# Attention in front of two expert layers: transposes on row halves, fp32 scores without parts, both products with v in one PSUM tile

## The chip, the cores and the metric

One core of a Trainium2 chip runs the whole program. The metric is the device time of one execution in microseconds; the median of three runs of the kernel before is 954.91 us (954.55 to 956.79).

## The reference

Three layers follow each other; only the first is touched by the change.

```python
B, H, S, D = q.shape                       # 4, 8, 576, 64
scores = q @ k^T / sqrt(D); scores = where(causal, -1e9, scores)
a = softmax(scores); local = a @ v
q_p = phi(q)                               # elu(q) + 1
mem_out = (q_p @ M_prev) / (q_p . z_prev + 1e-6)
g = sigmoid(beta)                          # per head
x = (g * mem_out + (1 - g) * local) -> [B*S, H*D] = [2304, 512]
...
# then: each token through one of 8 experts (512 -> 1024 -> 512), weighted by its gate,
# then elu(x @ w_in) @ w_out (512 -> 2048 -> 512)
```

## The kernel before, in words

The program has three stages, each planned and emitted by `Plan`: attention (with the routing of tokens to experts mixed in), the experts, the last layer. A stage is written as operations with an engine or a choice of engines, a cost, what they read and write, and a priority; `Plan.order` (L156) walks through time, gives each engine the next operation that is ready, hands out buffers from rings of fixed size, and so fixes the order of instructions on each engine. On the chip each engine then runs its list in that order. The costs are numbers in the source (`TICK`, `DRAIN`, `HOP`, and one per operation); the priorities are in the table `KNOBS`, `off` above all.

Attention goes through 16 pairs of heads (`pair(p)` in `attention`): 4 batches x 4 pairs. All its PSUM use goes through one ring of four buffers of 1024 fp32 columns, called `pat` in the trace (`c.rx`, two banks each). Per pair:

1. `load` (L543) brings q, k, v of both heads, 128 tokens to a row tile, so that a tile has 128 tokens x (2 heads x 64).
2. `tr` (L561) transposes k and q on TensorE, five 128x128 blocks each (L570), into PSUM: 128 partitions (2 heads x 64) x tokens.
3. `parts` (L574) reads these and writes two float32r parts of each, high and low: `ha` or `hv` (L584, L587) and a subtraction on VectorE (L591). `ends` (L632) copies the last 64 columns of q into a block-diagonal array (L641).
4. `phi_in` and the GpSimd step (L604 to L629) make phi(q).
5. `scores` (L653): row tiles of 128 queries i = 0 to 3, and a last one of 64 queries, both heads in one tile. Each score is a sum of three float32r matmuls, high x high, low x high, high x low (L667; L678 for the last tile). The two heads stand in the two halves of the array's rows. The causal mask is added by small bf16 matmuls (L671, L679). VectorE takes the row minimum (L687; scores are negated), ScalarE the exponential with its row sum (L692).
6. `weights` (L696): the weights are transposed on TensorE in 128x128 blocks (L705), 2, 4, 6, 8 and 5 of them for the five row tiles, and copied out of PSUM (`evac`, L515) into `aA` (tiles 0 to 2) and `aB` (tiles 3 and 4).
7. A matmul with `swap` (L750) brings one row sum to the other half; VectorE makes the factors (L754 to L762).
8. `quarters` (L522) multiplies phi(q) with the memory (64x64 quarters of the array, four at once), and later the transposed result with an identity to bring it back (same line).
9. The products with v (L806): 384 tokens from `aA`, 192 from `aB`, the two heads in the two halves of the array's columns, each group in its own PSUM buffer and copied on its own (`evac` to `xT`).
10. VectorE scales (L791, L826), GpSimd adds into the row of x (L838).

After each batch `gate_plan` computes which expert each token goes to (a table by 20 bf16 matmuls, L945, among others), and `routing` the places of the first tiles.

Of the kernel before, what the change touches and what calls it, by code (L numbers as in the profile page):

```python
# [18 lines left out]
P = 128  # L19
# [5 lines left out]
NI = 5  # L25
# [59 lines left out]

class Plan:
# [10 lines left out]
    DRAIN = 90.0  # L97
# [129 lines left out]
    "xe": ("ACT", "DVE"), "he": ("ACT",), "re": [("ACT",), ("ACT", "DVE")], "m_ld": 3500.0, "m_x": -2208.9, "m_1": -1447.9, "m_h": -4434.5,  # L227
    "m_lag": 0.0, "m_if": 700.0, "m_fl": -3000.0, "m_wl": 300.0, "wa": 0, "wa0": 10022.449169040721, "wa1": 23927.854833523612, "wt": 1, "wp": 16, "wj": 2000.0,
    "m_g": -500, "wq": 0.64, "sa": 60.0, "sm": 50.0, "s2": 0.0, "step": -68438.62, "hd": -241.62,
    "mem": 379947.52, "xg": 4,  # L230
# [242 lines left out]
def attention(tc, ctx, c, q, k, v, M_prev):  # L473
# [28 lines left out]
    r_aA, r_aB = sb("aA", 2, [P, 2, 896]), sb("aB", 2, [P, 2, NI, 192])  # L502
# [12 lines left out]
    def evac(n, dst, src, **kw):  # L515
# [5 lines left out]
        pl.op(("ACT", "DVE"), (ca(n), cv(n)), (fa, fv), **kw)  # L521
# [9 lines left out]
    def pair(p):  # L531
# [8 lines left out]

        def load(slot, src, lo, eng="SP"):
# [8 lines left out]
        load(sqi, q, D)  # L550
        load(ski, k, 0, "ACT" if p == 0 else "SP")
# [5 lines left out]
        def row(y):  # L557
            return sab.t[:, y * QW:(y + 1) * QW]

        def diag(x):  # L560
            return sab.t[:, 4 * QW + P * x:4 * QW + P * (x + 1)]  # L561
        xq, xk = [(Slot(rx), 0, QW)], [(Slot(rx), 0, S)]

        def tr(xs, s):
            pt = at("tk" if s is ski else "tq")
            for x, n0, n1 in xs:
                def mk(x, n0, n1):
                    def f():
# [3 lines left out]
                    pl.op("PE", 109 * -(-(n1 - n0) // P), f, r=[s], w=[x] + [(y, "own", n0) for y in ([sab] if s is ski else [sab, se, sqT])], prio=pt)  # L572
                mk(x, n0, n1)

        def parts(xs, hi, lo, scale):
            for x, n0, n1 in xs:
                def mk(x, n0, n1):
                    n = n1 - n0

                    def to(y):  # L580
                        return row(y)[:, n0:n1]

                    def ha():
                        nc.scalar.activation(to(hi), x.t[:, 0:n], AF.Copy, scale=scale)  # L584

                    def hv():
                        nc.vector.tensor_scalar_mul(to(hi), x.t[:, 0:n], scale)  # L587
                    pl.op(("ACT", "DVE"), (ca(n), cv(n)), (ha, hv), r=[x, (x, 0)], w=[(sab, hi)], prio=at("hi"))

                    def f():  # L590
                        nc.vector.scalar_tensor_tensor(to(lo), x.t[:, 0:n], scale, to(hi).bitcast(F32), op0=ALU.mult, op1=ALU.subtract)  # L591
                    pl.op("DVE", cv(n), f, r=[x, (sab, hi)], w=[(sab, lo), (x, 0)], prio=at("lo"))
                mk(x, n0, n1)

# [4 lines left out]
        parts(xk, 0, 2, 1.0)  # L599
        xq0 = xq[0][0]  # L600

        def phi_in():
            def f():
                nc.scalar.activation(se.t, xq0.t[:, 0:QW], AF.Exp)  # L604
            pl.op("ACT", ca(QW), f, r=[xq0], w=[se, (xq0, 0)], prio=at("px"))

            def f():
                nc.scalar.activation(sqT.t[:, 0:512], xq0.t[:, 0:512], AF.Relu)
            pl.op("ACT", ca(512), f, r=[xq0], w=[(sqT, 0), (xq0, 0)], prio=at("px"))

# [6 lines left out]
        parts(xq, 1, 3, -0.125)  # L617
# [3 lines left out]
        for n, n0, n1, m0 in ((0, 0, 512, 0), (1, 512, S, S)):  # L621
            def mk(n, n0, n1, m0):
                def fv():
                    nc.vector.scalar_tensor_tensor(sqT.t[:, n0:n1], se.t[:, m0:m0 + n1 - n0], 1.0, sqT.t[:, n0:n1], op0=ALU.min, op1=ALU.add)

                def fp():
                    e = se.t[:, m0:m0 + n1 - n0]
                    nc.gpsimd.tensor_scalar(e, e, 1.0, 0.0, op0=ALU.min, op1=ALU.add)  # L628
                    nc.gpsimd.tensor_tensor(sqT.t[:, n0:n1], e, sqT.t[:, n0:n1], op=ALU.add)  # L629
                es, m = K["qe"], n1 - n0  # L630
                pl.op(es, [{"DVE": cv(m), "POOL": cps(m) + cpt(m)}[x] for x in es], [{"DVE": fv, "POOL": fp}[x] for x in es], r=[se], w=[(sqT, n), (se, "phi", n)], prio=at("phi"))
            mk(n, n0, n1, m0)  # L632
# [64 lines left out]
        def weights(i, hs, js, ps):  # L697
# [12 lines left out]
            def dst():  # L710
# [3 lines left out]
                if i == 3:  # L714
                    return sB.t[:, h, j0:j1, 0:P]
# [1063 lines left out]
```

## Time and profile before

| what | value |
|---|---|
| median of three runs | 954.91 us |
| the profiled execution | 954.44 us, its span 952.7 us |
| PE (TensorE matmuls) busy | 921.3 us, 97% |
| PEld (TensorE weight loads) busy | 770.3 us, 81% |
| DVE (VectorE) busy | 639.2 us, 67% |
| ACT (ScalarE) busy | 446.9 us, 47% |
| POOL (GpSimd) busy | 179.6 us, 19% |
| granted TensorE clock, mean | 0.991 |

A line of the profile names engine, source line and operation, then output <- inputs by the program's names. For a TensorE line the pair like 64\*128 is the rows and columns of the array in use, and the next one the partitions and moving columns. An fp32 matmul that is not a transpose stands in the trace as two instructions, a float32r one, a bf16 one and a transpose as one. Matmuls are pipelined: a start-to-start distance is what one costs, its own length is more.

### The profile page before, as it was taken

What the parts mean: (1) busy time and instruction counts of PE and PEld (TensorE: products, weight loads), DVE (VectorE), ACT (ScalarE), POOL (GpSimd) and SP (SyncE); (2) the same over time, 40 slices, a digit from 0 to 9 for tenths busy, and PEclk for the clock granted to TensorE, in tenths of its full rate; (3) what the DMA queues carried; (4) which work ended last, traced back from release to release, by engine and by line L of the source; (5) the groups of instructions that cost most, each with busy time, mean ns of one, the idle gap of its engine ahead of it and who ended that gap; (6) DMA issues with size and microseconds to landing.
All of it is one profiled execution on the core that took longest, in us unless ns stands there. A gap on an engine that the chain in (4) does not pass through costs nothing. (4 is left out here: it accounts for less than half of the span.)

```text
span 952.7 us, 18441 instructions
## 1 busy us (share of the span) xinstructions
PE 921.3 (97%) x6858; PEld 770.3 (81%) x6858; DVE 639.2 (67%) x1179; ACT 446.9 (47%) x902; POOL 179.6 (19%) x244
## 2 busy tenths in 40 slices
PE   9998998999899999999999999999999999999996
PEld 6777887778678888888878789988888888888895
DVE  3878878887775568646898596555565556555553
ACT  3787778767454347536866562222122221212211
POOL 3344442434300122222321100010001000100100
PEclk8999999989999999999999999999999999999999
DMA  6333433243632697569997370110011000100000
GB/s 124 79 75 84 94 75 103 64 147 132 221 122 88 228 343 250 170 225 361 331 335 279 125 242 1 34 45 1 1 45 45 1 12 23 45 0 1 20 26 23
DMA packets 96597, 110.00 MB, mean 115 GB/s; under 512 B 64879, under 2 KB 64879, under 8 KB 94193
## 3 DMA queue, kind: packets, MB, share of 16 engines
q1 hardware_dynamic: 90496, 95.25, 31.4%
q0 software_dynamic: 4800, 13.18, 3.8%
q8 instruction: 55, 0.90, 0.4%
q10 hardware_dynamic: 1200, 0.30, 0.2%
q14 instruction: 46, 0.37, 0.1%
HBM read 87.94 MB, written 23.41 MB: 117 GB/s over the span
## 5 line engine op out<-in xcount | busy, mean ns | idle before, releaser
L1588 ACT ACTIVATE elu<-pt 128x512 f32<-128x512 f32 x72 | 43.1, 598 | 266.0 <-PE pt L1580 266.0
L1613 PE MATMUL pt<-w,gh 128*128 128x512 f32 x432 | 134.2, 392 | 0.5 <-DVE gh L1492 0.5
L1380 PE MATMUL pm<-w,hh 128*128 128x512 f32 x368 | 125.1, 401 | 0.8 <-ACT y L1393 0.8
L1596 DVE TENSOR_SCALAR elu<-elu 128x512 f32<-128x512 f32 x72 | 30.8, 428 | 127.1 <-ACT elu L1588 127.1
L1613 PEld LDWEIGHTS pt<-w,gh 128*128 128x128 f32 x432 | 79.6, 188 | 16.3 <-DVE gh L1492 0.9
L692 ACT ACTIVATE a<-pat,st 128x128 f32<-128x128 f32 (+2 forms) x144 | 78.0, 550 | 22.5 <-DVE st L687 18.3
L1613 PE MATMUL pt<-w,gl 128*128 128x512 f32 x216 | 84.3, 390 | 0.0
L1380 PEld LDWEIGHTS pm<-w,hh 128*128 128x128 f32 x368 | 69.2, 188 | 14.5 <-ACT y L1393 1.2
L1380 PE MATMUL pm<-w,hl 128*128 128x512 f32 x184 | 71.9, 391 | 0.3 <-DVE hl L1214 0.3
L687 DVE TENSOR_REDUCE st<-pat 128x2 f32<-128x256 f32 (+4 forms) x80 | 63.8, 806 | 9.6 <-PE pat L671 9.6
L1580 PE MATMUL pt<-yTh,w 128*128 128x256 f32 (+1 forms) x288 | 69.2, 319 | 0.0
L705 PE MATMUL pat<-ident,a 128*128 128x128 f32 x400 | 56.9, 287 | 8.6 <-ACT a L692 8.4
L628 POOL TENSOR_SCALAR ex<-ex 128x512 f32<-128x512 f32 (+1 forms) x32 | 37.8, 1182 | 131.0 <-ACT ex L604 118.5
L705 PEld LDWEIGHTS pat<-ident,a 128*128 128x128 f32 x400 | 44.6, 145 | 16.0 <-ACT a L692 15.0
L1600 DVE SCALAR_TENSOR_TENSOR tnh<-tnh,elu 128x512 f32<-128x512 f32 x72 | 49.6, 690 | 7.7 <-ACT tnh L1592 1.8
L1337 PE MATMUL pm<-w,x 128*128 128x512 f32 x216 | 51.9, 392 | 1.3 <-DVE w L1214 0.9
L1495 DVE TENSOR_TENSOR gl<-tnh,gh 128x512 fp32r<-128x512 f32 x72 | 49.6, 691 | 4.2
L1580 PEld LDWEIGHTS pt<-yTh,w 128*128 128x128 f32 x288 | 49.2, 190 | 4.0
L1604 DVE SCALAR_TENSOR_TENSOR tnh<-pt,tnh 128x512 f32<-128x512 f32 x72 | 49.6, 690 | 3.3
L1337 PEld LDWEIGHTS pm<-w,x 128*128 128x128 f32 x216 | 40.2, 188 | 10.3 <-DVE w L1214 1.4
L1214 DVE TENSOR_TENSOR hl<-pm,hh 128x512 fp32r<-128x512 f32 x46 | 31.4, 684 | 25.0 <-ACTq L1311 14.4
L1613 PEld LDWEIGHTS pt<-w,gl 128*128 128x128 f32 x216 | 40.5, 188 | 9.0 <-DVE gl L1495 0.4
(342 smaller groups left out, 2107.3 us busy)
## 6 DMA issues: line engine op xcount, KB each, us to landing
wraw<-in_moe_w_dram SPq DMA_DIRECT2D x24, 1024.0 KB, 7.9
wrbw<-in_moe_w_dram SPq DMA_DIRECT2D x12, 1024.0 KB, 8.1
wide<-in_moe_w_in_dram SPq DMA_DIRECT2D x16, 512.0 KB, 5.4
wf<-half SPq DMA_DIRECT2D x32, 256.0 KB, 3.2
wide<-in_moe_w_out_dram SPq DMA_DIRECT2D x16, 512.0 KB, 5.8
wide<-wf SPq DMA_DIRECT2D x9, 512.0 KB, 5.3
q<-in_q_dram SPq DMA_DIRECT2D x32, 128.0 KB, 3.1
v<-in_v_dram SPq DMA_DIRECT2D x32, 128.0 KB, 2.5
```

The source lines that it names most:

```text
L628: nc.gpsimd.tensor_scalar(e, e, 1.0, 0.0, op0=ALU.min, op1=ALU.add)
L687: nc.vector.tensor_reduce(ss.t[:, 2 * i:2 * i + (2 if i < 4 else 1)], src(), axis=AX.X if i < 4 else AX.XY, op=ALU.min)
L692: nc.scalar.activation(sa[i].t[:, h, :] if i < 4 else sa[4].t[:, 0:S].rearrange("p (y n) -> p y n", y=2), src()[:, h, :] if i < 4 else src ...
L705: nc.tensor.transpose(w.t[:, y:y + P], t[:, j * P:(j + 1) * P], c.ident)
L1337: nc.tensor.matmul(g[hf].t, a.t[:, cc, :], b[:, 512 * hf:512 * (hf + 1)], start=(cc == 0 and n == 0), stop=(cc == 3 and n == 2))
L1380: nc.tensor.matmul(y.t, a.t[:, 2 * (q % 2) + jj, :], b[:, 512 * jj:512 * (jj + 1)], start=(q == 0 and jj == 0 and n == 0), stop=(q == 3 an ...
L1495: nc.vector.tensor_sub(lo(), src(), hi().bitcast(F32))
L1580: nc.tensor.matmul(h.t[:, n * j + n0:n * j + n1], w(cc, a, ft), b(cc), start=(cc == 0 and x == 0), stop=(cc == 3 and x == 2))
L1588: nc.scalar.activation(se.t, h.t, AF.Exp)
L1600: nc.vector.scalar_tensor_tensor(st.t, st.t, 0.0, se.t, op0=ALU.min, op1=ALU.mult)
L1604: nc.vector.scalar_tensor_tensor(st.t, h.t, 0.0, st.t, op0=ALU.max, op1=ALU.add)
L1613: nc.tensor.matmul(acc[a].t, y.t[:, n * j + P * a:n * j + P * (a + 1)], wsub(1, k, ft // 2)[:, ft % 2, :], start=(ft == 0 and x == 0), sto ...
```

## The change

- q and k are loaded 64 tokens to a row tile: tokens 0 to 319 in partitions 0 to 63, tokens 320 to 575 in 64 to 127 (`halves`, four DMAs each).
- All transposes of attention go over 64 rows at a time (`turn`): a block of 64 tokens x 128 columns becomes 128 x 64, the two row halves in turn, each into its own PSUM bank.
- Scores are one fp32 matmul in place of three float32r ones, over the columns that exist (128 where 256 stood for the first tile). The low parts, the padded arrays and the block-diagonal copies go. The last tile works in two 64x64 quarters at a time.
- Both products with v go into one PSUM buffer, with the swap matmul in two halves between them, and are copied by one operation of 576 columns.
- phi(q) is made by operations of 576 columns in place of 512 and 64.
- `weights` are copied by engines that the table `es` names; the order of attention is planned anew.

```diff
+TURN = 32.5
+def turn(nc, out, x, ident, z):
+    hs = slice(z * D, (z + 1) * D)
+    nc.tensor.transpose(out, x, ident[hs, hs])
...
-    DRAIN = 90.0
+    DRAIN = 95.0
...
+    "es": {"x": ("ACT",), "T0": ("ACT", "DVE"), "T3": ("ACT", "DVE"), "k": ("DVE",), "T1": ("ACT",), "T4": ("ACT", "DVE"), "q": ("ACT",), "T2": ("ACT",)},
...
+                for h in range(2):
+                    e.dma_start(t[0:D, :, h, :], src[b, h0 + h, 0:n, :].rearrange("(i p) d -> p i d", p=D))
+                    e.dma_start(t[D:P, 0:NI - 1, h, :], src[b, h0 + h, n:S, :].rearrange("(i p) d -> p i d", p=D))
...
-                        for i in range(n0 // P, -(-n1 // P)):
-                            nc.tensor.transpose(x.t[:, i * P - n0:(i + 1) * P - n0], s.t[:, i, :, :].rearrange("p h d -> p (h d)"), c.ident)
+                for i in range(NI):
+                    for z in range(2 if i < NI - 1 else 1):
+                        n = 512 * z + (i - NI * (1 - z)) * D + 512 * (1 - z)
+                        turn(nc, x.t[:, n:n + D], s.t[z * D:(z + 1) * D, i, :, :].rearrange("p h d -> p (h d)"), c.ident, z)
...
-                        nc.vector.scalar_tensor_tensor(to(lo), x.t[:, 0:n], scale, to(hi).bitcast(F32), op0=ALU.mult, op1=ALU.subtract)
+                nc.scalar.activation(row(y), at_tokens(x), AF.Copy, scale=scale)
...
-                for k, (x, y) in enumerate(((0, 1), (2, 1), (0, 3))):
-                    for h in range(2):
-                        hs = slice(h * D, (h + 1) * D)
-                        nc.tensor.matmul(s.t[:, 512 * h:512 * h + m], row(y)[hs, i * P:(i + 1) * P], row(x)[hs, 0:m], start=(k == 0), stop=False)
+                for h in range(2):
+                    hs = slice(h * D, (h + 1) * D)
+                    nc.tensor.matmul(s.t[:, 512 * h:512 * h + n], row(1)[hs, i * P:(i + 1) * P], row(0)[hs, 0:n], start=True, stop=False)
...
-                    for k, (w, z) in enumerate(((0, 0), (2, 0), (0, 1))):
-                        nc.tensor.matmul(o, diag(z), row(w)[:, 288 * y:288 * (y + 1)], start=(k == 0), stop=(k == 2 and y == 0))
+                    for h in range(2):
+                        hs, z = slice(h * D, (h + 1) * D), (y + h) % 2
+                        nc.tensor.matmul(s.t[hs, 512 * z:512 * z + 288], row(1)[hs, 512:S], row(0)[hs, 288 * z:288 * (z + 1)], start=True, stop=(z == 0))
...
-                    nc.tensor.transpose(w.t[:, y:y + P], t[:, j * P:(j + 1) * P], c.ident)
+                    for z in range(2):
+                        turn(nc, w.t[:, 512 * z + y * D:512 * z + (y + 1) * D], t[z * D:(z + 1) * D, j * P:(j + 1) * P], c.ident, z)
...
+        wx = Slot(rw)
+        for g, (so, tiles, n, n0) in enumerate(((sA, (0, 1, 2), 384, P), (sB, (3, 4), 192, 512))):
...
+                        for h in range(2 * first):
+                            nc.tensor.matmul(wx.t[h * D:(h + 1) * D, 1000:1001], c.swap[:, h * D:(h + 1) * D], ss.t[:, 20:21], start=True, stop=True)
+                        for h in range(2):
+                            nc.tensor.matmul(wx.t[h * D:(h + 1) * D, n0 + o:n0 + n], svi.t[:, j, h, :], so.t[:, j, h, o:n], start=(j == 0), stop=(j == tiles[-1]))
...
+        evac("x", S, lambda: sx.t[:, 0:S], lambda: wx.t[:, P:P + S], r=[wx], w=[sx, (wx, "z")], prio=at("ave"))
```

The new plan moves work on every engine of the attention stage. On TensorE, in the middle of a pair (`pat` is a PSUM buffer; `a` the weights of one row tile, `k` and `q` those of the next pair), before:

```order
L705 MATMUL pat_95<-ident,a_210 128x128 x2
L705 MATMUL pat_94<-ident,a_212 128x128 x4
L570 MATMUL pat_95<-ident,k_198 128x128 x5
L705 MATMUL pat_96<-ident,a_214 128x128 x6
L705 MATMUL pat_94<-ident,a_218 128x128 x5
L705 MATMUL pat_97<-ident,a_216 128x128 x8
L750 MATMUL pat_95<-st_234,swap 128x1
L570 MATMUL pat_96<-ident,q_196 128x128 x5
L529 MATMUL pat_94<-mb,qpT_226 64x73 x20
L529 MATMUL pat_95<-iw,xT_232 64x72 x20
L806 MATMUL pat_97<-aA_222,v_206 64x384 x2
```

and of the change:

```order
L536 MATMUL pat_96<-mb,qpT_222 64x73 x20
L92 MATMUL pat_97<-ident,a_205 128x64 x4
L92 MATMUL pat_95<-ident,a_207 128x64 x8
L92 MATMUL pat_97<-ident,a_209 128x64 x12
L92 MATMUL pat_94<-ident,k_197 128x64 x9
L92 MATMUL pat_95<-ident,a_214 128x64 x10
L92 MATMUL pat_96<-ident,a_211 128x64 x16
L92 MATMUL pat_97<-ident,q_194 128x64 x9
L741 MATMUL pat_94<-aA_217,v_202 64x384 x2
L741 MATMUL pat_94<-aA_217,v_202 64x256 x2
L741 MATMUL pat_94<-aA_217,v_202 64x128 x2
L739 MATMUL pat_94<-st_230,swap 64x1 x2
```

The quarters, which stood between the transposes of q and the products with v, now stand ahead of the transposes (those with `iw` between the fourth and fifth score tile); the products follow the transposes of q at once, and k comes after the third tile's weights in place of the second's.

On ScalarE, from the exponentials of the last row tile to the copies of the products, before:

```order
L692 ACTIVATE a_218,st_234<-pat_94,st_234 128x576
L517 COPY aA_222<-pat_95 128x2x3x128
L517 COPY aB_224<-pat_96 128x5x2x64
L517 COPY aB_224<-pat_94 128x2x4x128
L604 ACTIVATE ex<-pat_95 128x640
L608 ACTIVATE qpT_228<-pat_95 128x512
L612 ACTIVATE qpT_228<-pat_95 128x64
L584 ACTIVATE ab_203<-pat_95 128x640
L517 COPY xT_230<-pat_94 128x384
L517 COPY xT_230<-pat_96 128x192
```

and of the change:

```order
L666 ACTIVATE a_214,st_230<-pat_94,st_230 128x576
L524 COPY aA_217<-pat_97 128x4x128
L524 COPY aA_217<-pat_95 128x6x128
L524 COPY aB_219<-pat_97 128x2x5x64
L524 COPY aB_219<-pat_96 128x8x128
L606 ACTIVATE ex<-pat_95 128x576
L610 ACTIVATE qpT_220<-pat_95 128x576
L593 ACTIVATE ab_198<-pat_95 128x576
L524 COPY xT_226<-pat_94 128x576
```

The copy of the second tile's weights (4 x 128 columns) has come to ScalarE from VectorE, and one relu and one copy of the products are gone from it.

On VectorE, in a pair of the change, from the first row minimum (L661) to the fifth:

```order
L661 TENSOR_REDUCE st_228<-pat_95 128x2
L748 COPY st_230<-pat_96 128x1
L752 SCALAR_TENSOR_TENSOR st_230<-st_230,omg 128x10
L661 TENSOR_REDUCE st_228<-pat_97 128x2
L756 RECIPROCAL st_230<-st_230 128x10
L661 TENSOR_REDUCE st_228<-pat_94 128x2
L661 TENSOR_REDUCE st_228<-pat_95 128x2
L773 TENSOR_TENSOR ls_237<-pat_96,st_230 128x2x5x72
L661 TENSOR_REDUCE st_228<-pat_97 128x1
```

Here the small work on row sums (L748 to L756) and the scaling of the products (L773) of the pair before stand among the minima; in the kernel before, the four wide minima follow each other, and this work comes after the transposes.

## Rows read from the trace of the kernel before

**Rows 1.** Timeline of PE at the stage's start and end (start us, us, line, names, shapes).

```profile
15.09 0.41 PE L356 MATMUL pat<-ident,wraw 32*64 32x32 f32 x2
17.25 1.01 PE L667 MATMUL pat<-ab 64*128 64x256 f32 x6
...
228.27 0.62 PE L667 MATMUL pat<-ab 64*128 64x256 f32 x6
...
243.24 1.66 PE L1337 MATMUL pm<-wq,x 128*128 128x512 f32 x6 [0.69 <-DVE ls L826]
```

**Rows 2.** Timeline of PE over one head pair.

```profile
114.56 0.62 PE L667 MATMUL pat<-ab 64*128 64x256 f32 x6
...
115.12 0.60 PE L667 MATMUL pat<-ab 64*128 64x256 f32 x6
...
115.65 0.77 PE L667 MATMUL pat<-ab 64*128 64x384 f32 x6
...
116.36 0.94 PE L667 MATMUL pat<-ab 64*128 64x512 f32 x6
...
117.33 1.06 PE L678 MATMUL pat<-ab 128*128 128x288 f32 x6
...
118.27 0.42 PE L705 MATMUL pat<-ident,a 128*128 128x128 f32 x2
...
120.27 2.36 PE L705 MATMUL pat<-ident,a 128*128 128x128 f32 x19 [0.22 <-ACT a L692]
122.47 0.28 PE L750 MATMUL pat<-st,swap 128*128 128x1 f32 x2
...
123.28 0.86 PE L529 MATMUL pat<-mb,qpT 64*64 64x73 f32 x40
...
124.70 1.52 PE L806 MATMUL pat<-aA,v 128*64 128x384 f32 x12
126.05 1.58 PE L806 MATMUL pat<-aB,v 128*64 128x192 f32 x20
127.56 0.39 PE L667 MATMUL pat<-ab 64*128 64x256 f32 x2
```

**Rows 3.** Windows: us, busy by engine (instructions), granted clock, DMA share, GB/s.

```profile
14.40:21.20 6.80, 6.80 (x48) 4.72 (x49) 2.48 (x8) 3.11 (x11) 3.92 (x4) 0.50 0.60 126
...
118.20:123.90 5.70, 5.32 (x76) 4.56 (x78) 4.18 (x9) 5.36 (x13) 0.00 (x0) 1.00 0.23 52
202.20:208.90 6.70, 6.11 (x41) 5.60 (x39) 5.37 (x27) 4.42 (x11) 0.00 (x0) 0.50 0.50 179
114.50:127.50 13.00, 12.62 (x202) 10.38 (x196) 10.35 (x20) 10.11 (x27) 5.88 (x8) 1.00 0.31 69
```

**Rows 4.** Waits of PE, 30 to 240 us: total us, times, longest.

```profile
PE pat L705 <- ACT a L692: 7.8, 25, 0.8
```

**Rows 5.** Timeline of PEld, windows cut after one, two, three (L667: two, four) loads.

```profile
105.23 0.14 PEld L705 LDWEIGHTS pat<-ident,a 128*128 128x128 f32 x1 [0.40 <-ACT a L692]
...
105.23 0.20 PEld L705 LDWEIGHTS pat<-ident,a 128*128 128x128 f32 x2 [0.40 <-ACT a L692]
...
105.23 0.31 PEld L705 LDWEIGHTS pat<-ident,a 128*128 128x128 f32 x3 [0.40 <-ACT a L692]
...
100.93 0.19 PEld L667 LDWEIGHTS pat<-ab 64*128 64x128 f32 x2
...
100.93 0.30 PEld L667 LDWEIGHTS pat<-ab 64*128 64x128 f32 x4
```

**Rows 6.** Groups of DVE by form, 30 to 240 us: busy us, mean ns, idle before.

```profile
L687 DVE TENSOR_REDUCE st<-pat 128x2 f32<-128x1024 f32 x15 | 18.3, 1220 | 0.0
...
L687 DVE TENSOR_REDUCE st<-pat 128x2 f32<-128x768 f32 x15 | 14.3, 954 | 0.0
...
L591 DVE SCALAR_TENSOR_TENSOR ab<-pat,ab 128x640 fp32r<-128x640 f32 x15 | 12.2, 814 | 0.0
L687 DVE TENSOR_REDUCE st<-pat 128x1 f32<-128x576 f32 x15 | 11.2, 745 | 0.0
L687 DVE TENSOR_REDUCE st<-pat 128x2 f32<-128x512 f32 x15 | 10.3, 688 | 2.0 <-PE pat L671 2.0
...
L591 DVE SCALAR_TENSOR_TENSOR ab<-pat,ab 128x576 fp32r<-128x576 f32 x13 | 9.8, 756 | 1.9 <-ACT ab L584 1.6
```

**Rows 7.** Timeline of ACT in the same pair: first exponential, end of the last, first copies.

```profile
115.78 0.37 ACT L692 ACTIVATE a<-pat,st 128x128 f32<-128x128 f32 x1 [0.78 <-DVE st L687]
...
120.73 0.21 ACT L692 ACTIVATION_READ_ACCUMULATOR a<-pat,st 128x1 f32 x1
121.18 0.80 ACT L517 COPY aA<-pat 128x768 f32<-128x768 f32 x1 [0.24 <-PE pat L705]
121.87 1.81 ACT L517 COPY aB<-pat 128x640 f32<-128x640 f32 x2
```

More of the change, by code (lines that the diff above doesn't have):

```diff
@@ L226 @@
 KNOBS = {
[L227 to L230, printed above, removed]
+    "xe": ("ACT", "DVE"), "he": ("ACT",), "re": [("ACT",), ("ACT", "DVE")], "m_ld": 3500.0, "m_x": -2208.9, "m_1": -1447.9, "m_h": -4434.5, "m_lag": 0.0,
@@ L513, in attention, with either, evac @@
     ORD, O = K["ord"], K["off"]
-    def evac(n, dst, src, **kw):
+    def either(name, cost, fa, fv, **kw):
+        es = K["es"].get(name, ("ACT", "DVE"))
+        pl.op(es, [cost[x] for x in es], [{"ACT": fa, "DVE": fv}[x] for x in es], **kw)
+    def evac(name, n, dst, src, **kw):
         def fa():
@@ L549, in load @@
             pl.op(eng, 1950, f, w=[slot], prio=pr - 3000, dma=1640)
-        load(sqi, q, D)
-        load(ski, k, 0, "ACT" if p == 0 else "SP")
+        halves(sqi, q)
+        halves(ski, k, "ACT" if p == 0 else "SP")
         load(svi, v, 0)
@@ L575, in parts @@
[L575 to L590, printed above, removed]
-                        nc.vector.scalar_tensor_tensor(to(lo), x.t[:, 0:n], scale, to(hi).bitcast(F32), op0=ALU.mult, op1=ALU.subtract)
-                    pl.op("DVE", cv(n), f, r=[x, (sab, hi)], w=[(sab, lo), (x, 0)], prio=at("lo"))
-                mk(x, n0, n1)
+            return sab.t[:, y * S:(y + 1) * S]
@@ L596, in pair, with part, fa, fv @@
+        def part(name, x, y, scale):
+            def fa():
+                nc.scalar.activation(row(y), at_tokens(x), AF.Copy, scale=scale)
+            def fv():
+                nc.vector.tensor_scalar_mul(row(y), at_tokens(x), scale)
+            either(name, {"ACT": ca(S), "DVE": cv(S)}, fa, fv, r=[x, (x, 0)], w=[(sab, y)], prio=at("h" + name))
         se, sqT = Slot(r_ex), Slot(r_qpT)
@@ L615, in pair @@
         if p:
             phi_in()
-        parts(xq, 1, 3, -0.125)
+        part("q", xq, 1, -0.125)
         if not p:
             phi_in()
[L621 to L632, printed above, removed]
@@ L732, in pair @@
         for o, i in enumerate(ORD):
-            ps = pr + K["step"] * o
-            if K["wide"]:
-                cut = [((0, 1) if i < 4 else (0,), tuple(range(i + 1)))]
-            elif i == 4:
-                cut = [((0,), (0, 1, 2, 3)), ((0,), (4,))]
-            elif i < 2:
-                cut = [((0, 1), tuple(range(i + 1)))]
-            else:
-                cut = [((h,), tuple(range(i + 1))) for h in range(2)]
-            for hs, js in cut:
-                weights(i, hs, js, ps + K["hd"] * hs[-1])
-                blocks += [(i, h, j) for h in hs for j in js]
@@ L761, in f3 @@
-        def f3():
-            nc.vector.reciprocal(ss.t[:, 12:22], ss.t[:, 12:22])
-        pl.seq("DVE", ((70, f), (90, f2), (115, f3)), r=[wz] + [(ss, "s", i, h) for i in range(NI) for h in range(2 if i < 4 else 1)] + ["g"], w=[(ss, "r")], prio=at("fin"))
+            weights(i, pr + K["step"] * o)
         sx, srn = Slot(r_xT), Slot(r_rn)
@@ L813, in pair @@
+        pl.seq("DVE", ((70, f), (200, f2), (200, f3)), r=[wx, (wx, "z")] + [(ss, "s", i, h) for i in range(NI) for h in range(2 if i < 4 else 1)] + ["g"], w=[(ss, "r")], prio=at("fin"))
         if hp == 0:
```

165 lines of the change are left out of this document (66 added, 99 removed).

## Prediction, made before the changed kernel was run

> **What bounds the kernel now.** I read the timeline of TensorE first, because the page has it busy nearly throughout. The change touches only the attention stage, which runs from 17.25 us (first score matmul) to 243.24 us (first matmul of the next stage) [rows 1]; the instructions behind it stand in the same order as before on every engine, so a gain there shifts the rest earlier as a whole. Sixteen head pairs pass, one after the other. From the first score matmul of one to that of the next it takes 13.0 us where no routing work falls in between (114.56 to 127.56) [rows 2]. The windows view of such a pair has PE busy 12.62 of 13.0 us, ACT 10.11, DVE 10.35 [rows 3]. So PE is the bound, and what it idles for is the chain through ACT: the waits view has 25 waits of the transposes for the exponentials, 7.8 us in all [rows 4].
>
> Where PE's 13.0 us go, from start to start [rows 2]: the four wide score tiles 114.56 to 117.33, **2.77**; the fifth 117.33 to 118.27, **0.94**; 25 transposes of weights and 5 of k, 118.27 to 122.47, 4.20, of which 30 x 0.109 = **3.27** is work (19 of them lie between 120.27 and 122.47 less a short group behind them: 19 x 0.109 = 2.07) and **0.93** is waiting; swap and 5 transposes of q to 123.28, **0.81**; the two groups of quarters to 124.70, **1.42**; both products with v to 127.56, **2.86**. Work 12.07, waits 0.93.
>
> **Transposes.** 35 blocks of 128x128 at 0.109 us, 3.82 us per pair, become 68 half blocks (50 of weights, 18 of k and q): a load of 64 rows x 128 columns and 64 moving columns, alternating between the row halves. No row shows one, so the price is bounded. Low end: a block moves 128 columns in 0.109 us; 64 take half, 0.054, and with both halves at work at once each costs **0.027**. That halves do work at once is seen in the scores: from the 256- to the 384-column tile the period grows from 0.53 to 0.71 us [rows 2], so 6 x 128 columns more take 0.18 us, 4.3 columns per ns, twice one column per clock at 2.4 GHz. High end: no overlap, and the load sets the pace. A transposing load frees its place after 0.06 us: where PE starts from rest, the stretch of one load ends 0.14 us after its start, of two 0.20, of three 0.31 [rows 5]. So loads follow by 0.06 where nothing moves and by 0.11 where 128 columns move between them. High end **0.060** per half. I take **0.0325**: both halves load together as the scores' loads do, 0.060 per two, and 0.005 for the alternation. 68 x 0.0325 = 2.21; saved 1.6 us per pair (low end 2.0; high end 4.08, 0.26 lost).
>
> The rule that speaks against this is in the Trainium skill, "TensorE: Matmul & The Clock Gate", section "LDWEIGHTS (loading the stationary operand)": a load takes columns / 1.2 ns, whatever the rows, so half the rows would cost the same. By it a half block would cost 0.107 / 2 = 0.053 us, 68 of them 3.64, and only 0.18 us per pair would be saved (an estimate from that page). The trace agrees for the ordinary loads of the scores (two more loads end 0.11 us later, 0.19 to 0.30) and not for transposing ones (0.06) [rows 5].
>
> **Scores.** Three terms at one clock per column become one fp32 matmul. Its rate is in the products with v: 768 columns per head in the first group took 1.35 us of 126.05 less 124.70 [rows 2], 1.76 ns per column, 4 clocks with little over. So (128 + 256 + 384 + 512) x 4 / 2.4 = 2.13 us against 3 x (256 + 256 + 384 + 512) / 2.4 = 1.76: +0.37, of which 0.05 goes with fewer restarts: **+0.32**. The fifth tile: 2 x 288 x 4 / 2.4 = 0.96 against 6 x 288 / 2.4 = 0.72 in a row of 0.94; less a block-diagonal load and mask, **+0.11**. Bounds for both together 0.3 and 0.6.
>
> **Products with v** keep their columns; the swap matmul moves into their tile: **-0.11**, bounded by 0 and its whole 0.14. The number of changes of array shape per pair stays four.
>
> PE's work per pair: 12.07 - 1.61 + 0.32 + 0.11 - 0.11 = **10.8 us**.
>
> **What PE then waits for.** I follow one pair with the durations of before; t = 0 is its first score matmul. Scores end at 0.34, 0.95, 1.77; the reductions on DVE (0.42, 0.69, 0.95, 1.22, 0.75 [rows 6]; the first by its columns) follow, with the small work on row sums now between the first two: 0.64 to 1.06, 1.45 to 2.1, 2.3 to 3.25. The fourth score tile reuses the first's PSUM buffer, freed by its exponentials at 2.0: it runs 2.05 to 3.1, its reduction 3.3 to 4.5. Quarters and fifth tile to 5.0; its reduction must wait for a multiply of 0.9 that now stands ahead of it: 5.33 to 6.05. The nine exponentials took 115.78 to 120.94 [rows 7]; here they end at 7.0, since the last starts at 6.2. The transposes start at 5.8 but need buffers that ACT and DVE free: 0.2 lost at each of the second and third group, and k can start only at 7.2, in the fifth tile's buffer. ACT then copies the weight tiles (768 columns take 0.69 to the next start [rows 7]; the others by their columns at that rate 0.48, 0.59, 0.90) to 9.67, and does exp, relu and the scaled q to 11.4. PE: transposes end 8.8, products 8.9 to 11.75, next pair at **11.85**. Of this 10.8 is work and 1.0 waits, against 12.07 and 0.93. **Gain 1.2 us per pair** (bounds: no wait left, 2.2 to 10.8; I allow 1.8; waits up by 0.7, 0.5).
>
> The removed low parts (0.81 for q, 0.76 for k [rows 6]) and the copies to the diagonal end a load of DVE that lay beside PE; only q's low part reached the end of a pair (it ran until just before 127.56), and the scaled q on ACT takes its place. I cost them at nothing beyond the above. The loads of q and k issue four DMAs each where three were: 64 more on SP, where each pair's stand a pair ahead; nothing, except for the first q, 0.1 us, in the start below. The GpSimd step becomes one op each of 576: it ends 2 us into the pair and its reader comes at 5.0.
>
> **Sum.**
> - 15 steps from pair to pair x 1.2 = 18.0 (bounds 7.5 and 27).
> - Start: the scores came at 17.25 [rows 1], after k, q, four products of constants, low parts and diagonal copies. Now q is transposed ahead of the second product, and the scores stand right behind it; it ended at 15.5 [rows 1], less 0.5 of transposes: 15.0. Gain 2.3 (0 to 2.8).
> - Excess: from the first pair's scores to the last's it takes 228.27 - 17.25 = 211.0 us [rows 1], 16 more than 15 x 13.0: three routing stages and two stretches at half clock [rows 3]. Their PE work is fixed; the waits within shrink as DVE loses 1.6 us of low parts per pair, and the new order puts the table's 20 matmuls where PE waits for buffers. I take 4 of 16 (0 to 8).
> - End: 243.24 - 228.27 = 15.0 for the last pair. Now 11.85 less the k and q turns, then the one copy of 576 ahead of all quarters (1.1), quarters 0.73, the last multiply 0.6: 14.3. Gain 0.7 (0 to 1.2).
>
> Together **25.0 us**. The profiled execution took 954.44 us (span 952.7), so 929.4; the median of the runs shown is 0.5 higher: **930 us**.
>
> **Rivals.**
> 1. *The buffers set the pace.* With PE quicker, the four PSUM buffers and ACT behind them are what ends last: my walk has five places within 0.2 us of each other, and ACT's work after the last exponential (4.4 us) plus the chain up to it (7.0) is already 11.4. If each hand-over costs 0.1 to 0.2 more, a pair takes 12.5: 15 x 0.5 + 2.3 + 2 + 0.3 = 12; **943 us**. Against: ACT was busy 10.11 of 13.0 us, with gaps [rows 3]. The Trainium skill, "TensorEngine Tiling (Array Packing)", section "PSUM Bottleneck", warns of this: tiling speeds up TensorE, not the emptying of PSUM. By that rule the gain would be cut as in this rival; the trace has the first signs, in the waits of rows 4.
> 2. *The halves do not overlap* (other side: slower). If a half's load waits for the other half's transpose, each costs its 0.060. PE's work is 12.07 + 0.26 + 0.32 = 12.65, with waits 13.6 per pair: 15 x 0.6 = 9 lost, 2 to 3 gained at the start: **961 us**. It decides from 0.052 us per half: there 68 halves save 0.28 less than the scores and fifth tile cost. For it: no transposes on alternating halves are in the trace. Against: the scores' overlap.
> 3. *The half block's load takes what the scores' loads take*, 0.107 us for 128 columns [rows 5], both halves together: 0.053 per half, work 12.07 - 0.18 + 0.32 = 12.2, waits as now, 13.1 per pair: 1.5 lost, 2.3 gained at the start: **953 us**, no change. Against: the 0.06 of the transposing loads. It is what the section of the Trainium skill named above, "LDWEIGHTS (loading the stationary operand)", would make of this kernel.
> 4. *The clock falls.* It stood at 1.2 GHz (0.50) from 202.2 to 208.9 us and at 2.4 GHz (1.00) from 118.2 to 123.9, where nothing but transposes and short waits stand [rows 3]. With fewer columns moving in that stretch it may fall more often. Each fall costs half of some 6.8 us; one per two pairs, 8 x 3.4 = 27, takes the gain: **957 us**.
>
> **How the numbers follow.** My forecast 0.74; rivals in order 0.12, 0.06, 0.04, 0.04. The upper bounds of its four terms add to 39 us and the lower to 7.5; not all at one end at once, I take 37 and 13, so 917 to 941; with the first rival the range is **917 to 945**, which leaves out the others, 0.14, and a little below. Faster by over 0.3% (3 us, about what a measurement of this kernel can tell from no change): 0.86; within: 0.04 (rival 3); slower: 0.10 (rivals 2 and 4).
>
> **What would show it.** Right: half blocks start 0.03 to 0.035 us apart; pairs without routing follow by 11.6 to 12.1 us; the first scores near 15 us; waits of PE on ACT and DVE among the transposes of about 1 us per pair. Wrong: spacings of 0.05 or more (rivals 2, 3); spacings right but pairs at 12.5 with PE idle for ACT copies (rival 1); a granted clock of 0.50 inside ordinary pairs (rival 4).

## The result, and the profile after

| | median, us | range | against before |
|---|---|---|---|
| before | 955.69 (4 runs) | 954.55 to 956.79 | |
| after | 939.39 (4 runs) | 938.11 to 943.06 | 0.9836 [0.9805, 0.9867] |

Faster by 16.3 us, where 25 were forecast; 939.4 lies inside the range. The profiled execution of the changed kernel is the highest of its four (943.06 us, span 941.3). In the two profiles the stage ends 243.24 - 231.51 = 11.7 us sooner.

PE at the stage's start and end, which answers to [rows 1] (start us, us, engine, line, names, shapes):

```profile
13.04 3.58 PE L364 MATMUL pat<-wraw,wraw 64*64 64x8 f32 x32
16.54 0.41 PE L365 MATMUL pat<-ident,wraw 32*64 32x32 f32 x2
16.89 0.80 PE L639 MATMUL pat<-ab 64*128 64x128 f32 x4
...
227.39 1.61 PE L741 MATMUL pat<-aB,v 128*64 128x192 f32 x20
229.79 0.86 PE L536 MATMUL pat<-iw,xT 64*64 64x72 f32 x40 [0.78 <-ACT xT L524]
231.51 1.66 PE L1284 MATMUL pm<-wq,x 128*128 128x512 f32 x6 [0.87 <-DVE ls L773]
```

PE over one ordinary pair, which answers to [rows 2]:

```profile
108.95 0.49 PE L639 MATMUL pat<-ab 64*128 64x128 f32 x4
...
112.09 0.86 PE L536 MATMUL pat<-iw,xT 64*64 64x72 f32 x40
112.99 1.19 PE L650 MATMUL pat<-ab 64*64 64x288 f32 x8
...
114.18 0.86 PE L536 MATMUL pat<-mb,qpT 64*64 64x73 f32 x40
114.98 0.34 PE L92 MATMUL pat<-ident,a 64*128 64x64 f32 x4
115.47 0.96 PE L92 MATMUL pat<-ident,a 64*128 64x64 f32 x20 [0.16 <-ACT a L666]
116.28 0.57 PE L92 MATMUL pat<-ident,k 64*128 64x64 f32 x9
116.76 1.03 PE L92 MATMUL pat<-ident,a 64*128 64x64 f32 x26
117.62 0.48 PE L92 MATMUL pat<-ident,q 64*128 64x64 f32 x9
118.03 1.51 PE L741 MATMUL pat<-aA,v 128*64 128x384 f32 x12
119.38 0.23 PE L739 MATMUL pat<-st,swap 128*64 128x1 f32 x4
119.47 1.61 PE L741 MATMUL pat<-aB,v 128*64 128x192 f32 x20
121.01 0.38 PE L639 MATMUL pat<-ab 64*128 64x128 f32 x2
```

The pair takes 121.01 - 108.95 = 12.06 us, and five pairs of the middle, those without routing work, take 12.05 or 12.06. All 68 half blocks pass in 3.05 us, 114.98 to 118.03. The windows (columns as in [rows 3]) show that pair, and three stretches at half clock (granted 0.50 and 0.51, so 1.2 GHz):

```profile
108.95:121.01 12.06, 11.85 (x230) 8.74 (x226) 7.91 (x14) 10.16 (x26) 5.53 (x6) 1.00 0.31 70
...
10.80:21.10 10.30, 10.30 (x89) 8.61 (x89) 3.09 (x8) 3.56 (x11) 3.55 (x2) 0.50 0.44 93
85.90:89.30 3.40, 3.40 (x58) 2.39 (x56) 2.13 (x2) 2.75 (x10) 0.61 (x2) 0.51 0.32 72
191.70:195.20 3.50, 3.50 (x64) 2.52 (x62) 2.13 (x2) 2.72 (x10) 0.78 (x2) 0.51 0.07 17
```

PE's waits, which answer to [rows 4] (30 to 225 us): the transposes' waits on the exponentials fell from 7.8 to 1.9 us, and a wait of the widest score tile on a row minimum, three times, is new:

```profile
PE pat L639 <- DVE st L661: 7.0, 3, 2.5
PE pat L92 <- DVE aA L527: 2.1, 4, 0.7
PE pat L92 <- ACT a L666: 1.9, 11, 0.3
```

So the 11.7 us are: start 17.25 - 16.89 = 0.4; 15 steps x (13.0 - 12.06) = 14.1; the excess over 15 equal steps 16.0 before and 215.99 - 16.89 - 15 x 12.06 = 18.2 now, -2.2; end 15.0 before and 231.51 - 215.99 = 15.5 now, -0.5. (215.99 is the last pair's first score matmul.)

### The profile page after: what moved, and what is told of

Read it like the earlier page. It is cut to its first block, busy times and chain, and to the rows that moved or that the text cites. A ratio compares the mean times of both kernels' runs of the same rounds, so it can differ in the third digit from the quotient of the medians.

```text
span 941.3 us, 19282 instructions
## 1 busy us (share of the span) xinstructions
PE 906.4 (96%) x7334; PEld 743.4 (79%) x7334; DVE 606.9 (64%) x1104; ACT 447.7 (48%) x879; POOL 174.7 (19%) x208
## 5 line engine op out<-in xcount | busy, mean ns | idle before, releaser
L661 DVE TENSOR_REDUCE st<-pat 128x2 f32<-128x256 f32 (+4 forms) x80 | 62.6, 793 | 50.1 <-PE pat L643 47.9
L639 PE MATMUL pat<-ab 64*128 64x128 f32 (+3 forms) x256 | 50.5, 492 | 7.2 <-DVE st L661 7.0
L1161 DVE TENSOR_TENSOR hl<-pm,hh 128x512 fp32r<-128x512 f32 x46 | 31.4, 685 | 25.5 <-ACTq L1258 14.4
L621 POOL TENSOR_SCALAR ex<-ex 128x576 f32<-128x576 f32 x16 | 34.2, 2135 | 68.2 <-ACT ex L606 68.2
L1527 PE MATMUL pt<-yTl,w 128*128 128x256 f32 (+1 forms) x144 | 45.8, 318 | 0.0
```

The source lines that it names most:

```text
L639: nc.tensor.matmul(s.t[:, 512 * h:512 * h + n], row(1)[hs, i * P:(i + 1) * P], row(0)[hs, 0:n], start=True, stop=False)
L661: nc.vector.tensor_reduce(ss.t[:, 2 * i:2 * i + (2 if i < 4 else 1)], src(), axis=AX.X if i < 4 else AX.XY, op=ALU.min)
L1527: nc.tensor.matmul(h.t[:, n * j + n0:n * j + n1], w(cc, a, ft), b(cc), start=(cc == 0 and x == 0), stop=(cc == 3 and x == 2))
```

## The experiments

Three runs ask what an ordinary pair waits for, three more test the answer, and two ask what bounds the pair then; the rest go to the routing, the end and the kernel before. Times are medians.

**Scores cheaper** (e4_one: 941.22 us, 0.9869 [0.9833, 0.9905]). The low parts of the wide scores are left out.

```diff
-row(1)[hs, i * P:(i + 1) * P], row(0)[hs, 0:n]
+row(1)[hs, i * P:(i + 1) * P], row(0)[hs, 0:max(n, 256)]   # both float32r
```

> The changed kernel with the four wide score tiles from one fp32r product of the rounded k and q (at least 256 columns): the low parts of the scores are left out. It takes (128+256+384+512) x 4 / 2.4 GHz less (256+256+384+512) / 2.4 GHz = 1.5 us of PE out of each pair. Theory: PE bounds the pair as it stands, but its exponentials are next: scores that come 1.5 us sooner meet ACT, busy 10.16 of 12.06 us, so 0.5 to 1.0 us per pair come through, 923 to 931 us. Rival 1 of the prediction (the buffers set the pace already): under 0.3 us per pair, 935 us or more. If nothing but PE counted: 12.06 - 1.5, 915 us.

Pairs stayed at 12.05 us: first score matmuls at 91.97, 104.03 and 116.08. 1.5 us less of PE per pair gave nothing: in PE's timeline they became two waits for buffers that ACT's exponentials free:

```profile
93.89 0.50 PE L639 MATMUL pat<-ab 64*128 64x512 f32 x2 [0.77 <-ACT a L666]
...
96.01 1.19 PE L650 MATMUL pat<-ab 64*64 64x288 f32 x8 [0.74 <-ACT a L666]
```

So **PE did not bound the changed kernel's pair**, though it was busy 11.85 of 12.06 us. The theory fell.

**Whole blocks for the weights** (e3_whole: 955.98 us, 1.0007 [0.9990, 1.0024]).

```diff
-for z in range(2):
-    turn(nc, w.t[:, 512 * z + y * D:...], t[z * D:(z + 1) * D, j * P:(j + 1) * P], c.ident, z)
+nc.tensor.transpose(w.t[:, y * P:(y + 1) * P], t[:, j * P:(j + 1) * P], c.ident)
```

> The changed kernel with the weights transposed in whole blocks again (25 of 128x128 per pair instead of 50 halves; k and q stay in halves), same planner costs, same order. Theory: PE bounds the pair, so 25 x (0.109 - 0.062) = 1.2 us more per pair show in full: pairs of 13.1 to 13.3 us, 956 to 959 us, no faster than the kernel before. Rival (PSUM buffers and ACT set the pace): ACT's exponentials and copies release the buffers at the same times, half or more of the 1.2 us is covered: pairs of 12.1 to 12.6 us, 940 to 948 us.

Pairs of 12.99 us (112.83 to 125.82): 0.93 more, just under the theory's 13.1. More time in the weights' transposes shows, less time in the scores does not. Work that is added can become the bound; so this run doesn't say what the bound was before.

**One half after the other** (e2_halves: 944.11 us, 0.9893 [0.9865, 0.9921]).

```diff
-for y in range(nb):
-    for z in range(2):
+for z in range(2):
+    for y in range(nb):
```

> The changed kernel with the half blocks of a transposed tile taken one row half after the other instead of in turn; same planner costs, same order of everything else. Theory: a half block is cheap (0.031 us) only because the other row half loads and multiplies at the same time; in a row on one half each costs its own load, 0.054 to 0.060 us, 68 x 0.025 = 1.7 to 2.0 us more of PE per pair. With PE busy in 11.85 of 12.06 us nothing covers it: pairs of 13.7 to 14.1 us, 965 to 971 us. Rival: the pace is that of a 64-column transposing load whatever the half before it, and alternating gives nothing: 939 us, 0.031 us per half as now.

A miss: 0.18 us per pair instead of 1.7 to 2.0. PE's timeline of this run shows why:

```profile
115.24 0.27 PE L92 MATMUL pat<-ident,k 64*128 64x64 f32 x1
115.29 0.29 PE L92 MATMUL pat<-ident,a 64*128 64x64 f32 x2
115.35 0.47 PE L92 MATMUL pat<-ident,k 64*128 64x64 f32 x8
```

In the program all of `a`'s half blocks come ahead of all of `k`'s. On the chip the first of `k` starts before the last two of `a`, which use the other row half: the halves run side by side whatever the order, within a few instructions. So that halves overlap is shown; that it needs the order in turns is not.

**What the loop is.** VectorE and GpSimd of the changed kernel in the pair above:

```profile
109.63 0.42 DVE L661 TENSOR_REDUCE st<-pat 128x2 f32<-128x256 f32 x1 [3.97 <-PE pat L643]
109.97 0.15 DVE L748 COPY st<-pat 128x1 f32<-128x1 f32 x1
110.16 1.07 DVE L752 SCALAR_TENSOR_TENSOR st<-st,omg 128x10 f32<-128x10 f32 x1
111.14 0.68 DVE L661 TENSOR_REDUCE st<-pat 128x2 f32<-128x512 f32 x1
```

```profile
107.58 2.13 POOL L621 TENSOR_SCALAR ex<-ex 128x576 f32<-128x576 f32 x1 [2.85 <-ACT ex L606]
109.80 1.40 POOL L622 TENSOR_TENSOR qpT<-ex,qpT 128x576 f32<-128x576 f32 x1
```

L752 handles ten numbers per partition. Its median over the 16 pairs is 1.06 us; the same step took 0.17 in the kernel before. It ends 0.03 us after GpSimd's L622, here and in ten other pairs, and the second row minimum stands behind it. That closes a loop over pairs: exponential of q on ACT and both GpSimd steps, 106.82 to 111.2, 4.4; second minimum to its exponential at 111.92, 0.7; the exponentials to 116.13, 4.2; the weights' copies to the next exponential of q at 118.88, 2.75. Together 118.88 - 106.82 = 12.06. ACT's part of it:

```profile
111.92 0.47 ACT L666 ACTIVATE a<-pat,st 128x256 f32<-128x256 f32 x1 [1.02 <-DVE st L661]
...
116.13 1.28 ACT L524 COPY aA<-pat 128x512 f32<-128x512 f32 x2
...
118.88 0.67 ACT L606 ACTIVATE ex<-pat 128x576 f32<-128x576 f32 x1
```

From 111.92 to 118.88 ACT has no idle time, so here it waits neither for scores nor for transposes. Where the transposes take longer, in e3_whole, the copies do wait for them (0.36 and 0.17 us in its pair). PE meets the loop at the fifth score tile, whose buffer the second tile's exponentials free: they end at 112.93, and its first matmul stands at 112.99. Three runs take the loop apart.

**Another form of L752** (e5_form: 943.03 us, 0.9870 [0.9855, 0.9885]).

```diff
-nc.vector.scalar_tensor_tensor(sm, sm, 1.0e-9, c.omg[...].to_broadcast([P, NI, 2]), ...)
+for h in range(2):
+    nc.vector.tensor_scalar(sm[:, :, h], sm[:, :, h], 1.0e-9, c.omg[:, h0 + h:h0 + h + 1], ...)
```

> The changed kernel with the small step on the row sums (L752, 128x10, two inputs in SBUF) written as two steps of one tensor and one number per partition; its place in VectorE's order stays. Theory: after the change this step takes 1.06 us (median; 0.17 in the kernel before) because it runs into GpSimd's second feature step and waits until that ends; the second row minimum stands behind it, so exponentials, transposes, the copies and the next pair's features follow late, a loop of 12.05 us that TensorE's scores are no part of. Without the second SBUF input it takes 0.2 to 0.4 us, the second row minimum comes 0.6 to 0.8 us sooner, and the pair falls to what TensorE needs, 11.6 to 11.8 us: 932 to 935 us. Rival: the long step waits for nothing but its own inputs, or the loop runs elsewhere (ACT's copies and PSUM buffers): pairs stay at 12.05 us, 938 to 941 us.

A miss: pairs of 12.17 to 12.20 us. The two steps take 0.22 us each where nothing holds them, but here 1.32 together, until GpSimd's L622 (107.98 for 1.40) has ended:

```profile
108.23 1.32 DVE L753 TENSOR_SCALAR st<-st,omg 128x5 f32<-128x5 f32 x2
109.46 0.68 DVE L661 TENSOR_REDUCE st<-pat 128x2 f32<-128x512 f32 x1
```

The number of tensor inputs was the wrong handle.

**L752 one place later** (e9_fin: 936.77 us, 0.9807 [0.9786, 0.9827]), GpSimd untouched:

```diff
-"fin": -811685.9
+"fin": 0.0
```

> The changed kernel with GpSimd's feature step left where it is, and only the small step on row sums (L752) one place later in VectorE's order: behind the second row minimum instead of ahead of it (one number of the planner; beside it only buffer numbers and a few later places differ). Theory: what the loop of 12.05 us needs is the second row minimum standing behind an instruction that GpSimd holds up. Moved, L752 waits 0.4 us or less, the second minimum starts right behind the first, and ordinary pairs take 11.6 to 11.8 us as with the feature step on VectorE: 931 to 936 us. Rival (the gain of the feature step on VectorE came from the earlier end of the feature step itself, or from the routing steps): pairs of 12.0 us, 937 to 941 us.

Pairs of 11.72 us (105.25 to 116.97), as expected; the median lies 0.8 us above the range. The place of one instruction of ten numbers is worth 0.34 us per pair.

```profile
106.47 0.69 DVE L661 TENSOR_REDUCE st<-pat 128x2 f32<-128x512 f32 x1
107.07 0.45 DVE L752 SCALAR_TENSOR_TENSOR st<-st,omg 128x10 f32<-128x10 f32 x1
```

**The feature step on VectorE** (e6_phi: 929.99 us, 0.9740 [0.9726, 0.9753]).

```diff
-nc.gpsimd.tensor_scalar(e, e, 1.0, 0.0, op0=ALU.min, op1=ALU.add)
-nc.gpsimd.tensor_tensor(sqT.t[:, 0:S], e, sqT.t[:, 0:S], op=ALU.add)
+nc.vector.scalar_tensor_tensor(sqT.t[:, 0:S], se.t[:, 0:S], 1.0, sqT.t[:, 0:S], op0=ALU.min, op1=ALU.add)
```

> The changed kernel with the feature step (minimum with 1, addition) as one VectorE instruction of 576 instead of two on GpSimd. It takes VectorE 0.7 us per pair, which stands idle some 4 us of 12, and ends the feature step 2.5 us sooner. Theory: with GpSimd's feature steps gone, neither the small step on row sums (1.06 us) nor the routing table's steps (up to 1.49 us where 0.28 is usual) are held up: pairs of 11.6 to 11.8 us, and the pairs behind a routing stage 1 to 1.5 us shorter: 928 to 934 us. Rival (ACT and the PSUM buffers set the pace of 12.05 us): 0.7 us more on VectorE and no gain, 938 to 943 us.

As the theory had it, and faster than both kernels. L752 takes 0.17 us again, the new step 0.76:

```profile
102.16 0.76 DVE L620 SCALAR_TENSOR_TENSOR qpT<-ex,qpT 128x576 f32<-128x576 f32 x1 [2.35 <-ACT qpT L610]
103.71 0.42 DVE L661 TENSOR_REDUCE st<-pat 128x2 f32<-128x256 f32 x1 [0.79 <-PE pat L643]
...
104.23 0.17 DVE L752 SCALAR_TENSOR_TENSOR st<-st,omg 128x10 f32<-128x10 f32 x1
104.32 0.68 DVE L661 TENSOR_REDUCE st<-pat 128x2 f32<-128x512 f32 x1
```

Pairs take 11.60 us. PE over one of them: scores, quarters and fifth tile, transposes, products, next pair:

```profile
103.09 0.49 PE L639 MATMUL pat<-ab 64*128 64x128 f32 x4
...
106.17 0.86 PE L536 MATMUL pat<-iw,xT 64*64 64x72 f32 x40
...
108.62 0.34 PE L92 MATMUL pat<-ident,a 64*128 64x64 f32 x4
...
111.72 1.52 PE L741 MATMUL pat<-aA,v 128*64 128x384 f32 x12
...
114.70 0.49 PE L639 MATMUL pat<-ab 64*128 64x128 f32 x4
```

**Is PE the bound now?** Two runs on top of it ask.

> The changed kernel with the feature step on VectorE and the weights transposed in whole blocks (25 of 128x128 per pair instead of 50 halves). Theory: with the loop gone TensorE bounds the pair and the 25 x (0.109 - 0.062) = 1.2 us of the whole blocks come on top of 11.6 us: pairs of 12.7 to 12.9 us, 946 to 951 us, so the half blocks of the weights alone are worth 16 to 20 us. Rival (ACT's copies and the buffers set 11.6 us): under 12.2 us per pair, 940 us or less.

e11_wholephi (the diffs of e6_phi and e3_whole): 946.84 us, 0.9914 [0.9891, 0.9937]. Pairs of 12.74 us (109.60 to 122.34), 1.14 more: all of the transposes' cost shows. The weights' half blocks are worth 946.84 - 929.99 = 16.9 us.

> The feature step on VectorE and, together with it, the wide score tiles from one fp32r product (their low parts left out), which alone changed nothing. Theory: with the loop through GpSimd and the row sums gone, TensorE is the bound again, and the 1.5 us of products that the scores lose now show until ACT's 10.2 us and its waits end last: pairs of 10.8 to 11.3 us, 6 to 14 us less than with the feature step alone. Rival (another loop without the scores sets the pace, through ACT's copies and the buffers): within 3 us of the run with the feature step alone.

e7_phione (the diffs of e6_phi and e4_one; the low parts left out again): 925.61 us, 0.9684 [0.9670, 0.9699]. Pairs of 10.99 us, 0.6 less, where the same edit gave nothing before. By the medians 4.4 us less, under the 6 expected; from the first scores to the stage's end 213.76 - 16.83 = 196.9 us against 219.06 - 14.74 = 204.3, so 7.4 less. The profiled start was 2.1 us later, at half clock. So PE was the bound, but by 0.6 us only: of the 1.5 us taken from it no more came through. ACT is now close: busy 10.14 of 10.99 us.

**Routing.** In the changed kernel VectorE's order has the routing table's steps ahead of the next pair's first row minimum, and GpSimd holds them too. VectorE and then GpSimd behind the first routing stage:

```profile
80.67 0.68 DVE L870 TENSOR_SCALAR raw<-col,grq 128x128 bf16<-128x128 f32 x1
80.86 0.56 DVE L873 TENSOR_SCALAR qone<-col,grq 128x144 bf16<-128x144 f32 x1
81.34 1.49 DVE L870 TENSOR_SCALAR raw<-col,grq 128x128 bf16<-128x128 f32 x1
...
83.66 0.41 DVE L661 TENSOR_REDUCE st<-pat 128x2 f32<-128x256 f32 x1
```

```profile
79.11 2.16 POOL L621 TENSOR_SCALAR ex<-ex 128x576 f32<-128x576 f32 x1 [3.63 <-ACT ex L606]
81.35 1.40 POOL L622 TENSOR_TENSOR qpT<-ex,qpT 128x576 f32<-128x576 f32 x1
```

The widest score tile then starts at 84.96, after a wait of 2.17 us, and from 86.0 us the clock is at half.

```diff
-"gate": -157676.6
+"gate": 200000.0
```

> The changed kernel with the routing step's small operations ordered behind the five row minima of the pair that follows (one number of the planner). Theory: after the change these operations stand ahead of the first row minimum, so the 512-column score tile waits for its PSUM buffer (7.0 us of PE waits on DVE's row minimum in the changed kernel's trace) and the clock falls behind two of the three stages. Expected: those waits under 1 us, the pairs behind a routing stage shorter by 1 to 2 us each, 932 to 936 us against 939.4. Rival: the routing chain only moves its waits elsewhere (the table's transposes and products hold a PSUM buffer longer): 938 to 941 us.

e1_gate (that number alone): 940.54 us, 0.9850 [0.9826, 0.9874], the rival's time; its reason, a PSUM buffer held longer, is not shown. The waits on the minimum and both stretches at half clock are gone. But the four steps from the sixth pair's scores (80.80 in the changed kernel, 78.71 here, to 134.20 and 131.59) take 52.9 us against 53.4: the steps now stand ahead of VectorE's scaled copy of k, and run into GpSimd's additions (L859 took 0.93 us, L870 0.83).

> The feature step on VectorE and the routing step's small operations behind the five row minima of the next pair. Theory: what remains of the routing stages' excess (some 16 us over 15 equal pairs) is the 512-column score tile waiting for a row minimum behind these operations; with both, 925 to 930 us, 2 to 4 us less than with the feature step alone. Rival: moved, the routing steps make later waits as long as those they end, as the move alone showed (no gain): within 1.5 us of the run with the feature step alone.

e8_phigate (the diffs of e6_phi and e1_gate): 935.30 us, 0.9793 [0.9777, 0.9809], 5.3 us more than e6_phi. A further miss: moved, the routing steps cost more than where they were. In e6_phi the same four steps take 127.43 - 77.31 = 50.1 us with the old place, at full clock: it was the hold by GpSimd that made the place bad.

**Two that told little.** e9_end (e6_phi, and two copies in the last pair): 931.65 us, 0.9759 [0.9737, 0.9780].

```diff
-evac("x", S, lambda: sx.t[:, 0:S], lambda: wx.t[:, P:P + S], r=[wx], ...)
+evac("x", 384, lambda: sx.t[:, 0:384], lambda: wx.t[:, P:512], r=[(sx, "own", 0, 2)], ...)
+evac("x", 192, lambda: sx.t[:, 384:S], lambda: wx.t[:, 512:P + S], r=[wx], ...)
```

> The changed kernel with the feature step on VectorE and, in the last pair alone, the copy of both products with v in two again (384 columns as soon as the first product is done, then 192), so that three fifths of the last quarters don't wait for the second product. Theory: the change put one copy of 576 columns between the last product and all quarters; in two, the stage ends 0.4 to 0.8 us sooner after the last pair's first scores: 929 to 930 us, a difference that only the trace can show. Rival: the last quarters wait for their row sums or a buffer all the same: no difference in the trace either.

From the last scores to the stage's end it took 221.50 - 206.19 = 15.3 us, against 219.06 - 204.28 = 14.8 with one copy: the second product now waits 0.62 us for the first copy, from the same PSUM tile. The rival, and a little worse.

e10_before (the kernel before): 980.63 us, 1.0267 [1.0240, 1.0295].

```diff
-"qe": ("POOL",)
+"qe": ("DVE",)
```

> The kernel before the change with its feature step on VectorE instead of GpSimd. Theory: the kernel before has no such meeting (the same small step takes 0.17 us there in nearly every pair) and is bound by TensorE, busy 12.62 of 13.0 us: pairs of 12.9 to 13.2 us, 952 to 958 us, no difference. Rival (GpSimd's feature step cost the kernel before as much, so it is no part of what the change lost): 950 us or less.

Neither: the planner laid out a different order, with two pairs' scores next to one another and 9.7 us of score tiles waiting for exponentials. It does not tell what GpSimd cost the kernel before; that it held L752's counterpart little is in the trace (0.17 us median; 0.39 twice, where it met a GpSimd step).

## Why the prediction was right in sign and short by a third

- **Transposes: right.** In the raw starts most half blocks come in pairs, 0 to 8 ns apart, and within a tile a pair mostly follows the one before it by 0.060 to 0.065 us: 0.031 per half (0.0325 taken). The second pair of a tile of weights comes 0.11 us after its first. Rivals 2 and 3 are refuted by that, and by e11_wholephi (25 blocks cost 1.14 us more than 50 halves, forecast 25 x (0.109 - 0.065) = 1.1).
- **PE's work per pair, 10.8: right.** In e6_phi, without the loop, the scores take 106.17 - 103.09 = 3.08 us (2.77 + 0.32 forecast), the quarters and the fifth tile 108.62 - 106.17 = 2.45 (1.42 + 1.05), the products with the swap 114.70 - 111.72 = 2.98 (some 3.0). The 68 half blocks take 3.10: 2.1 at 0.031 each and 1.0 in starts of tiles and waits, of which the trace names 0.15. So the work is 10.6, and 1.0 comes on top, as forecast (10.8 and 1.0).
- **The step of 1.2 us per pair: 0.94.** (13.0 - 11.85 is 1.15; it was rounded up.) In the changed kernel the quarters and the fifth tile take 114.98 - 112.09 = 2.89 us, 0.44 more than in e6_phi, and this is nearly all of the 0.46 between their pairs. What failed is the walk's path to the second row minimum. Of the feature step it says "The GpSimd step becomes one op each of 576: it ends 2 us into the pair and its reader comes at 5.0". It ends at 111.2, 2.25 us into the pair, as said, and its reader did not wait. What was missed stands in the walk: "with the small work on row sums now between the first two". That work was given 0.4 us; it met GpSimd and took 111.14 - 109.97 = 1.17, so the second minimum started 2.2 us into the pair instead of 1.45. Moving one instruction gave back 0.34 (e9_fin, where the quarters and the fifth tile take 2.45 again: 108.40 to 110.85), the feature step on VectorE 0.46 (e6_phi). The pair of 12.06 lies inside the 11.6 to 12.1 named as a sign of being right; with this loop in it, that is luck.
- Rival 1 had the kind right (something other than PE sets the pace) and the place wrong: the buffers and ACT allow 11.0, as e7_phione shows, and the waits in which it saw first signs fell from 7.8 to 1.9 us.
- "So PE is the bound", said of the kernel before, rested on its busy share; no run tests it.
- **Excess, 4 gained: -2.2**, the term that failed most in this profile, 6.2 us (the pairs 3.9), and outside its own bounds, 0 to 8. "the waits within shrink as DVE loses 1.6 us of low parts per pair" left out that VectorE's table steps would meet GpSimd: 7.0 us of new waits and two falls of the clock. In e6_phi the excess is 204.28 - 14.74 - 15 x 11.60 = 15.5: even without the hold only 0.5 of the 4 comes, and why the waits within did not shrink was not settled.
- **Start, 2.3: 0.4 in this profile, right in most others.** Here the clock fell at 10.9 us instead of 14.4, and 32 matmuls of the constants took 3.58 us. In eight of the eleven other profiles of the changed kernel's versions the first scores came at 14.2 to 14.9 us, a gain of 2.3 to 3.1; in one at 15.3, in two at 16.8. What decides when the clock falls was not settled.
- **End, 0.7: -0.5**, outside its bounds, 0 to 1.2. 15.5 us; 14.8 without GpSimd's hold. The one copy is waited for (0.78) as forecast, but the pair ahead of it was longer.
- Rival 4: no granted clock under 1.00 in ordinary pairs; the falls came behind two of the three waits of 2.2 to 2.5 us in routing.

That 939.4 lies inside the range is owed to the range's width: in the profile all four terms came short. That e6_phi lands on 930 us is a coincidence of terms: its pairs gain 15 x 1.4 = 21, its excess and end 0.7, its start 2.5.

## What to carry to other kernels

When a change reorders work, list for each engine not only what it waits for but what it runs beside: a VectorE step of 0.2 us that starts during a GpSimd step of 1.4 can take all of that, and whatever stands behind it is late. A busy share of 98% doesn't make an engine the bound; the test is to take work from it and see whether the period moves. (To add work tells less: what is added can become the bound.) Close the loop over iterations with numbers (here 4.4 + 0.7 + 4.2 + 2.75, some 12.05) before trusting a sum of one engine's work.

## What the hardware showed that was not expected

- Small VectorE steps whose inputs lie in SBUF (128x5 to 128x144) took up to 1.49 us where 0.17 to 0.29 is usual, when they ran into a GpSimd step. Inside GpSimd's addition L622 this was so for L752 in every pair where the addition had over 0.1 us to go; each time it ended 0.03 us after it. Inside L621 it was so in parts only: the routing steps near its start took 0.51 to 0.65 us, those in its last 0.6 us 0.56 to 0.69, the others their usual time; and L752 itself took 0.17 three times in e1_gate with 0.38 us of L621 to go. Row minima, which read PSUM, were not held (106.47 in e9_fin, 0.69 us inside L622).
- The Trainium skill, "SBUF — State Buffer", section "Who interferes with whom", states that VectorE and GpSimd share a pair of SBUF ports as an exclusive lock, held for a whole instruction, for VectorE steps with two SBUF inputs and for copies and scalar steps in a two-port mode. The trace agrees for L752, which has two inputs, inside L622 (1.06 us). L870 and e5_form's L753, of one tensor and a number per partition, were held too (1.49 us; 1.32 for two); whether they ran in a two-port mode no run here shows. Inside L621 the trace differs, as told above: some steps went through in their usual time, L752 among them.
- Transposes of one row half start ahead of earlier ones of the other half (e2_halves: `k` at 115.24 before the last of `a` at 115.29). So on TensorE the order of the list holds only to within a few instructions when these use different row halves.
